# Value products of a pair of heads: second head first, the first head's ordered behind it

## The chip, the cores and the metric

The kernel runs on one core of a Trainium2 chip (trn2). The metric is the time of one execution on the device in microseconds. Before the change the median of three runs is 677.95 us (675.8 to 678.87).

The engines are named as the profile names them: PE is TensorE (its matmuls; PEld its weight loads), DVE is VectorE, ACT is ScalarE, POOL is GpSimd, SP is the engine whose queue issues the transfers.

## The reference

Three layers follow each other, for 4 batches of 576 positions. The first is causal attention with 8 heads of width 64 and a decaying bias, and it is the one that the change touches:

```python
scores = scale * np.matmul(q, k.transpose(0, 1, 3, 2))
cum = np.cumsum(np.maximum(s, 0.0), axis=-1)
bias = -(cum[:, :, :, None] - cum[:, :, None, :])
scores = np.where(causal, -1000000000.0, scores + np.minimum(bias, 0.0))
attn = np.exp(scores - np.max(scores, axis=-1, keepdims=True))
attn = attn / (np.sum(attn, axis=-1, keepdims=True) + 1e-09)
return np.matmul(attn, v)
```

The second layer is a gated expert (512 to 1024 wide, a gelu, a normalization, a product over positions `w_sg`, a product `w_out`, a residual). The third mixes neighbouring positions, has a product `w_k` with a squared relu, a product `w_v`, and a gate `w_r`.

## The kernel before

**Attention in pairs.** `attn_pair(b, hp)` treats two heads of a batch, so there are 16 pairs, numbered 0 to 15, four to a batch. For each block of 128 queries it makes the scores of a head (`sc`, lines 255 and 256, two matmuls each), VectorE adds the mask and finds the minimum (line 280), ScalarE takes the exponent and the row sums (line 288), TensorE transposes the result (`tp`, lines 303, 306 and 314), and ScalarE or VectorE copies it into the pair's probabilities `pt1` and `pt2` (lines 308 to 317). The steps run first over head 0, then over the last 64 queries of both heads, then over head 1.

**The value products** (lines 328 to 341) come last. They have two stages: `r = 0` makes the first 256 query columns from two blocks of keys, `r = 1` the other 320 from five blocks. In a stage each block of keys has one product for each head: the weights are the head's values (128 keys by 64), the moving operand its probabilities, and the result goes to partitions 0 to 63 of the accumulator `pv` for head 0 and to 64 to 127 for head 1. A first stage therefore has 4 products (256, 256, 128 and 128 columns), a second stage 10 (six of 320, two of 192, two of 64). ScalarE then copies the accumulator into `x_t` (line 343), and later VectorE multiplies it by the reciprocals of the row sums (line 355). The sums reach that place by a transpose (`rt`, line 320), an addition and a reciprocal on VectorE, and a trip through memory (`rdram`).

**The other work.** `moe1(b)` is the second layer of a batch. `gemm3` (line 371) issues all its matmuls: `v`, `u`, `sg` (the product over positions, the gating product below) and `o`. The attention of a batch is emitted in pieces between the matmuls of the layer two of the batch before, by the due times of `attention_until`. When attention has ended, its memory goes to the weights of the third layer, whose products `k`, `r` and `ps` fill the rest of the span.

**What sets the order.** The code is not run as it is written: a scheduler puts each engine's instructions in an order of its own, by simulated times, the dependences between tiles, and the order of emission where several could go. Its result is what an engine then works through from first to last. `after(late, early)` adds a dependence without a semaphore: `late` may not stand ahead of `early` on their engine.

Of the kernel before, what the change touches and what calls it, by code (L numbers as in the profile page):

```python
# [38 lines left out]
def fused_kernel(ctx, tc, kqT, vL, s, w_in, g_ln, w_sgT, b_sg, w_out, mu_k, mu_r, w_k, w_v, w_r, out):  # L39
    nc = tc.nc  # L40
# [170 lines left out]
    def attn_pair(b, hp):  # L211
# [3 lines left out]
        for hh in range(2):  # L215
# [24 lines left out]
            if hh == 0:  # L240
                vf = at.tile([P, 2, NT, D], F32, tag="vf", name=f"vf{pr}", bufs=2)
# [18 lines left out]
        for hh, i in steps:  # L260
# [8 lines left out]
            for ci, (c0, c1) in enumerate(chunks):  # L269
                sc = psum1.tile([P, 512], F32, tag="sc", name=f"sc{pr}_{hh}_{i}_{ci}", bufs=3)  # L270
                n = c1 - c0
# [58 lines left out]
        for r in range(2):  # L330
            q0, n = ((0, QS), (QS, S - QS))[r]
            acc = psum1.tile([P, 512], F32, tag="acc", name=f"pv{pr}_{r}", bufs=3)
            nk = 2 if r == 0 else NT
            for kk in range(nk):
                o = max(0, kk * P - q0)
                for a in range(2):
                    if r == 0:
                        pt = pt1[:, a, :QS] if kk == 0 else pt1[:, a, QS:]
                    else:
                        pt = pt2[:, a, kk, o:] if kk < 4 else pt2[:, a, 3, 0:64]  # L340
                    nc.tensor.matmul(acc[64 * a:64 * a + 64, o:n], vf[:, a, kk], pt, start=(kk == 0), stop=(kk == nk - 1))  # L341

            nc.scalar.copy(x_t[:, q0:q0 + n], acc[:, :n])  # L343
            yield 4000
# [144 lines left out]
    def after(late, early):  # L489
        tc.add_manual_dep(late.ins, early.ins.name, mybir.DependencyInfo(mybir.DependencyClass.NoSync, mybir.DependencyReason.DATA),  # L490
                          reason="order")
# [23 lines left out]


    pairs = [attn_pair(b, h) for b in range(B) for h in range(H // 2)]

    def a_stream():
# [83 lines left out]
    def dense(name, w, x, m, n):  # L603
        acc = bank(name)
        f = slice(m * P, (m + 1) * P)
        mms = []
        for k in range(KD):
            xh, xl = (x[:, i, k, :n] for i in range(2))
            mms += [(w[0][:, k, f], xh), (w[0][:, k, f], xl), (w[1][:, k, f], xh)]
        gemm3(acc[:, :n], mms)  # L610
        return acc[:, :n]
# [57 lines left out]
    for c, (t0, n) in enumerate(TILES):  # L669
        nxt = mixed(c + 1, 0, lk) if c + 1 < len(TILES) else mixed(0, 1, lk)  # L670
        for hg in range(4):
            t = kp.tile([P, 2, CH], F32, tag="t", name=f"k2_{c}_{hg}", bufs=2)[:, :, :n]
            for i in range(2):
                acc = dense(f"k{c}_{hg}_{i}", wk, x, 2 * hg + i, n)
# [66 lines left out]
    for c, (t0, n) in enumerate(TILES):  # L741
# [9 lines left out]
        for h in range(2):  # L751
            g = va.tile([P, 2, CH], F32, tag="g", name=f"g{c}_{h}", bufs=2)[:, :, :n]
            for i in range(2):
                acc = dense(f"r{c}_{h}_{i}", wr, x, 2 * h + i, n)
# [21 lines left out]
    for p in range(TOK // PW):  # L776
# [7 lines left out]
        a, b, c = (psum2.tile([P, 2, 512], F32, tag="ps", name=f"ps{n}_{p}", bufs=4) for n in "abc")  # L784
# [80 lines left out]
```

## Time and profile before

| | |
|---|---|
| median of three runs | 677.95 us (675.8 to 678.87) |
| profiled execution | 676.04 us, its span 674.3 us |
| TensorE matmuls | 639.1 us (95%), 3912 records |
| VectorE | 476.5 us (71%) |
| ScalarE | 413.5 us (61%) |
| GpSimd | 216.9 us (32%) |
| value products (line 341) | 448 records, 65.2 us busy, from 28.4 to 373.4 us |

Busy times on TensorE overlap (a matmul's recorded end is modelled, and the next one has begun by then), so how long a group really took is read from its start to the start of what follows, or from the chain of waits, whose pieces do not overlap. The granted clock is 1.00 from 60 us on; before, it is at the lower level for a part of the time.

### The profile page before, as it was taken

To read this page: it belongs to the slowest core of one execution; us is meant where nothing else is said; L and a number is where in the kernel's file an instruction comes from. 1 tells how busy PE (TensorE), PEld (TensorE's weight loads), DVE (VectorE), ACT (ScalarE), POOL (GpSimd) and SP (SyncE) were. 2 spreads that over 40 slices of the span, in tenths; PEclk is the share of its full clock that TensorE was granted. 3 is DMA by queue.
4 is the path that set the end of the run, shared out by engine and by line. 5 is a ranking of instruction groups with operands and counts; after the bars stand their busy time and mean duration, and the time that the engine had idled before them with its cause. 6 is when DMAs were issued, how large, how long until landed. Compare 5 with 4: busy or idle time off the path is not lost.

```text
span 674.3 us, 11528 instructions
## 1 busy us (share of the span) xinstructions
PE 639.1 (95%) x3912; PEld 553.3 (82%) x3912; DVE 476.5 (71%) x995; ACT 413.5 (61%) x940; POOL 216.9 (32%) x233
## 2 busy tenths in 40 slices
PE   2769999899999999999999999999999999999997
PEld 1556777779878988978988889988888988999997
DVE  6877489997668735559744388887875959677773
ACT  5868787884558646458643376577755779543530
POOL 7546636657446378345454030000000000000000
PEclk9879999999999999999999999999999999999999
DMA  7566563544654550842600674576645594546543
GB/s 221 149 200 210 140 194 88 167 141 154 182 173 109 151 140 22 239 150 72 158 29 7 238 275 164 155 229 222 243 163 184 182 359 146 172 179 201 222 141 117
DMA packets 56459, 112.74 MB, mean 167 GB/s; under 512 B 7680, under 2 KB 20624, under 8 KB 56400
## 3 DMA queue, kind: packets, MB, share of 16 engines
q1 hardware_dynamic: 56400, 112.01, 52.1%
q8 instruction: 31, 0.51, 0.3%
q14 instruction: 28, 0.23, 0.1%
HBM read 74.46 MB, written 28.02 MB: 152 GB/s over the span
## 4 chain that ended last, share of the span: by engine, by line
PE 57%; DMA 4%; DVE 2%; ACT 1%; issue 0%; SPq 0%; POOL 0%; DVEq 0%
PE k L371 14%; PE r L371 7%; PE psa L774 7%; PE sg L371 6%; PE o L371 4%; PE psb L774 4%; PE pv L341 3%; PE u L371 2%; PE v L371 2%; PE psc L774 2%; PE tp L306 2%; DMA wc<-wscr 2%; PE sc L255 1%; PE sc L256 1%; DMA lraw<-in_w_k_dram 1%; DMA rdram<-rc 0%
## 5 line engine op out<-in xcount | busy, mean ns | idle before, releaser
L371 PE MATMUL k<-x,wk 128*128 128x512 f32 (+1 forms) x480 | 99.1, 368 | 0.0
L371 PEld LDWEIGHTS k<-x,wk 128*128 128x128 f32 x480 | 83.6, 189 | 15.2 <-ACT x L599 0.3
L255 PE MATMUL sc<-ka,qa 128*128 128x512 f32 (+3 forms) x180 | 62.6, 361 | 20.6 <-ACT wv L88 11.7
L288 ACT ACTIVATE st<-st,mx 128x128 f32<-128x128 f32 (+4 forms) x124 | 71.9, 582 | 11.9 <-DVE mx L280 10.4
L280 DVE CUSTOM_DVE_ANT_0 st<-sc,mask 128x512 f32<-128x512 f32 (+3 forms) x124 | 60.7, 501 | 17.7 <-PE sc L256 8.7
L341 PE MATMUL pv<-pt,vf 128*64 128x320 f32 (+4 forms) x448 | 65.2, 367 | 0.3 <-ACT xT L343 0.3
L371 PE MATMUL sg<-wsg,vn 128*128 128x288 f32 x448 | 64.0, 298 | 0.0
L371 PEld LDWEIGHTS sg<-wsg,vn 128*128 128x128 f32 x448 | 60.4, 188 | 0.6 <-DVE pt L310 0.2
L255 PEld LDWEIGHTS sc<-ka,qa 128*128 128x128 f32 x180 | 33.3, 187 | 31.3 <-ACT wv L88 11.7
L256 PE MATMUL sc<-KB,QB 128*128 128x512 f32 (+3 forms) x180 | 56.8, 337 | 0.5 <-DMA KB<-crt 0.5
L341 PEld LDWEIGHTS pv<-pt,vf 128*64 128x64 f32 x448 | 35.1, 137 | 24.7 <-issue 7.6
L306 PE MATMUL tp<-ident,st 128*128 128x128 f32 x300 | 49.5, 282 | 3.0 <-DVE pt L317 2.6
L371 PE MATMUL r<-x,wr 128*128 128x512 f32 (+1 forms) x240 | 49.5, 368 | 0.0
L371 PE MATMUL v<-wv,xs 128*128 128x512 f32 x192 | 49.1, 399 | 0.1
L371 PEld LDWEIGHTS r<-x,wr 128*128 128x128 f32 x240 | 41.9, 189 | 7.5
L70 POOL TENSOR_TENSOR KB<-kq,ka 64x576 fp32r<-64x576 f32 x29 | 43.6, 1503 | 9.7 <-DVE ka L233 3.4
L70 POOL TENSOR_TENSOR qa<-kq,QB 64x576 fp32r<-64x576 f32 x29 | 43.7, 1507 | 4.6 <-ACT QB L232 2.5
L306 PEld LDWEIGHTS tp<-ident,st 128*128 128x128 f32 x300 | 37.3, 145 | 8.7 <-ACT pt L308 3.9
L371 PE MATMUL u<-xs,wc 128*128 128x288 f32 x288 | 42.5, 298 | 1.1 <-DMA wc<-wscr 1.1
L232 POOL CAST QB<-kq 64x576 fp32r<-64x576 f32 x28 | 19.4, 692 | 73.0 <-PE sc L256 48.5
L371 PE MATMUL o<-gh,wc 128*128 128x288 f32 x192 | 40.8, 298 | 0.3 <-DMA wc<-wscr 0.3
L371 PEld LDWEIGHTS v<-wv,xs 128*128 128x128 f32 x192 | 34.9, 188 | 7.4 <-DVE y L480 0.5
(188 smaller groups left out, 1451.3 us busy)
## 6 DMA issues: line engine op xcount, KB each, us to landing
wc<-wscr SPq DMA_DIRECT2D x24, 512.0 KB
kq<-in_kqT_dram SPq DMA_DIRECT2D x32, 288.0 KB
kr<-kdram SPq DMA_DIRECT2D x12, 768.0 KB
kdram<-k SPq DMA_DIRECT2D x16, 512.0 KB
yt<-ydram SPq DMA_DIRECT2D x24, 257.0 KB
vf<-in_vL_dram SPq DMA_DIRECT2D x16, 320.0 KB
ydram<-y SPq DMA_DIRECT2D x16, 288.5 KB
gt<-gdram SPq DMA_DIRECT2D x12, 384.0 KB
```

What stands on the lines that cost most here:

```text
L70: eng.tensor_tensor(out=lo, in0=x, in1=f32(hi), op=ALU.subtract)
L232: (nc.scalar.copy if hd < 2 else nc.gpsimd.tensor_copy)(qb[64:128], kq[64:128])
L255: nc.tensor.matmul(sc[:m, :c1 - c0], qa[:, q], ka[:, c0:c1], start=True, stop=False)
L256: nc.tensor.matmul(sc[:m, :c1 - c0], qb[:, q], kb[:, c0:c1], start=False, stop=True)
L280: mi = nc.vector.tensor_tensor_reduce(out=st[:, c0:c1], in0=sc[:, :n], in1=mk, op0=ALU.add, op1=ALU.min, scale=-SCALE, scalar=mx[:, 0:1] i ...
L288: e = nc.scalar.activation(st[:, :w], st[:, :w], AF.Exp, bias=mx[:, last:last + 1], scale=-1.0, accum_out=sm[:, i + 5 * (hh == 1):i + 5 * ...
L306: nc.tensor.transpose(tp[:, c:c + P], st[:, j * P:(j + 1) * P], ident)
L341: nc.tensor.matmul(acc[64 * a:64 * a + 64, o:n], vf[:, a, kk], pt, start=(kk == 0), stop=(kk == nk - 1))
L371: nc.tensor.matmul(acc, a, w_, start=(i == 0), stop=(i == n - 1))
L774: nc.tensor.matmul(ps[:, c, :HW], l, r, start=(start and i == 0), stop=(i == len(mms) - 1), skip_group_check=True)
```

## The change

For each block of keys the product of head 1 is emitted first and that of head 0 second, and a dependence without a semaphore keeps head 0's behind head 1's on TensorE. This holds for both stages and all 16 pairs. Products of different blocks, other work between two products, and everything else are left to the scheduler as before.

```diff
-                for a in range(2):
+                both = []
+                for a in (1, 0):
                     if r == 0:
                         pt = pt1[:, a, :QS] if kk == 0 else pt1[:, a, QS:]
                     else:
                         pt = pt2[:, a, kk, o:] if kk < 4 else pt2[:, a, 3, 0:64]
-                    nc.tensor.matmul(acc[64 * a:64 * a + 64, o:n], vf[:, a, kk], pt, start=(kk == 0), stop=(kk == nk - 1))
+                    both.append(nc.tensor.matmul(acc[64 * a:64 * a + 64, o:n], vf[:, a, kk], pt, start=(kk == 0), stop=(kk == nk - 1)))
+                after(both[1], both[0])
```

Two lines are added, so line 341 of the kernel before is line 342 of the changed one, and line 371 is line 373.

The first place is TensorE around the value products of pair 14, with 16 pairs in all. `pv14_0` and `pv14_1` are the accumulators of its first and second stage, `sc15` scores of the next pair, `tp14` a transpose, `rt14` the transpose of the sums, `sg2` the gating product of batch 2. Before:

```order
L341 MATMUL pv14_0_4286<-pt1_14_4085,vf14_4070 64x256
L255 MATMUL sc15_2_4_0_4470<-ka31_4398,qa31_4397 128x512
...
L306 MATMUL tp14_1_3_4270<-ident_66,st14_1_3_4243 128x128 x4
L341 MATMUL pv14_0_4286<-pt1_14_4085,vf14_4070 64x256
L341 MATMUL pv14_0_4286<-pt1_14_4085,vf14_4070 64x128 x2
...
L341 MATMUL pv14_1_4308<-pt2_14_4086,vf14_4070 64x320
L255 MATMUL sc15_2_4_1_4476<-ka31_4398,qa31_4397 128x64
...
L341 MATMUL pv14_1_4308<-pt2_14_4086,vf14_4070 64x320 x5
L341 MATMUL pv14_1_4308<-pt2_14_4086,vf14_4070 64x192 x2
L341 MATMUL pv14_1_4308<-pt2_14_4086,vf14_4070 64x64 x2
```

The same place now:

```order
L306 MATMUL tp14_1_3_4270<-ident_66,st14_1_3_4243 128x128 x4
L342 MATMUL pv14_0_4286<-pt1_14_4085,vf14_4070 64x256 x2
L342 MATMUL pv14_0_4286<-pt1_14_4085,vf14_4070 64x128 x2
L320 MATMUL rt14_4276<-ident_66,sums0_96 9x128
L373 MATMUL sg2_0_1_4292<-wsg0_99,vn0_2_3645 128x288
...
L342 MATMUL pv14_1_4308<-pt2_14_4086,vf14_4070 64x320 x6
L342 MATMUL pv14_1_4308<-pt2_14_4086,vf14_4070 64x192 x2
L342 MATMUL pv14_1_4308<-pt2_14_4086,vf14_4070 64x64 x2
```

In each stage one product stood apart, ahead of the others; now both stages stand in one piece, behind the last transposes of head 1. In the order before, a product stands apart in the first stage of pairs 0, 3, 4, 5 and 9 to 15 and in the second stage of pairs 0, 1, 2, 3, 4, 8, 9, 12, 13 and 14, and pair 7's second stage is cut after five products. In the order now, only pair 7's second stage is cut, after six.

The second place is TensorE at the start of pair 8's scores. `sc8_0_0_0` is their first accumulator, `tp7` and `tq7` are transposes of pair 7, `sg0_0_1` and `sg0_1_0` gating products of batch 0. Before:

```order
L341 MATMUL pv6_1_1782<-pt2_6_1524,vf6_1508 64x320 x6
L341 MATMUL pv6_1_1782<-pt2_6_1524,vf6_1508 64x192 x2
L341 MATMUL pv6_1_1782<-pt2_6_1524,vf6_1508 64x64 x2
L306 MATMUL tp7_2_4_1958<-ident_66,st7_2_4_1942 128x128 x4
L314 MATMUL tq7_1963<-ident_66,st7_2_4_1942 128x128
L255 MATMUL sc8_0_0_0_2193<-ka16_2167,qa16_2166 128x128
L256 MATMUL sc8_0_0_0_2193<-KB0_90,QB0_88 128x128
```

The same place now:

```order
L306 MATMUL tp7_0_3_1936<-ident_66,st7_0_3_1912 128x128 x4
L255 MATMUL sc8_0_0_0_2193<-ka16_2167,qa16_2166 128x128
L373 MATMUL sg0_0_1_1766<-wsg0_99,vn0_0_1030 128x288
...
L342 MATMUL pv6_1_1782<-pt2_6_1524,vf6_1508 64x320 x6
L342 MATMUL pv6_1_1782<-pt2_6_1524,vf6_1508 64x192 x2
L342 MATMUL pv6_1_1782<-pt2_6_1524,vf6_1508 64x64 x2
L306 MATMUL tp7_2_4_1958<-ident_66,st7_2_4_1942 128x128 x4
L314 MATMUL tq7_1963<-ident_66,st7_2_4_1942 128x128
L256 MATMUL sc8_0_0_0_2193<-KB0_90,QB0_88 128x128
```

The first matmul of pair 8's scores has moved ahead of 14 gating matmuls, of pair 6's second stage and of five transposes; its second matmul has stayed behind them.

## Rows read from the trace of the kernel before

**Rows 1.** The page: busy us, share of the span, instructions.

```profile
PE 639.1 (95%) x3912; PEld 553.3 (82%) x3912; DVE 476.5 (71%) x995; ACT 413.5 (61%) x940; POOL 216.9 (32%) x233
```

**Rows 2.** Stretches: length, each engine's busy us, TensorE's granted clock, DMA share, GB/s.

```profile
28.00:84.00 56.00, 47.03 (x292) 33.95 (x291) 39.01 (x100) 41.76 (x115) 34.35 (x28) 0.90 0.58 174
...
100.00:160.00 60.00, 55.45 (x383) 47.49 (x382) 56.10 (x137) 48.40 (x136) 37.88 (x38) 1.00 0.49 148
160.00:375.00 215.00, 214.30 (x1465) 182.70 (x1465) 126.58 (x340) 119.19 (x308) 114.06 (x121) 1.00 0.41 119
```

**Rows 3.** TensorE's waits (sum, times, longest): 28-160, 160-375, 376-674 us.

```profile
PE sc L255 <- DVE mx L280: 6.4, 6, 3.0
PE tp L306 <- DVE pt L317: 2.6, 1, 2.6
...
PE sc L255 <- POOL xs L70: 0.4, 1, 0.4
PE pv L341 <- ACT xT L343: 0.3, 1, 0.3
...
PE u L371 <- DMA wc<-wscr: 1.1, 1, 1.1
```

**Rows 4.** The chain of waits around pair 14: start, length, what.

```profile
338.15 0.58 PE pv L341 x2
...
340.28 0.80 PE pv L341 x5
...
343.25 0.68 PE pv L341 x2
...
344.72 2.20 PE pv L341 x16
```

**Rows 5.** TensorE in order of time, pairs 7 and 10: start, length, what.

```profile
165.91 0.87 PE L341 MATMUL pv<-pt,vf 128*64 128x256 f32 x8
166.71 0.40 PE L371 MATMUL o<-gh,wcs 128*128 128x288 f32 x1
...
170.79 1.83 PE L341 MATMUL pv<-pt,vf 128*64 128x320 f32 x10
172.54 0.53 PE L371 MATMUL o<-gh,wcs 128*128 128x288 f32 x2
173.01 1.19 PE L341 MATMUL pv<-pt,vf 128*64 128x320 f32 x10
174.13 0.44 PE L306 MATMUL tp<-ident,st 128*128 128x128 f32 x2
...
245.26 2.27 PE L341 MATMUL pv<-pt,vf 128*64 128x320 f32 x20
247.46 0.80 PE L371 MATMUL sg<-wsg,vn 128*128 128x288 f32 x4
```

**Rows 6.** The chain of waits: three transposes at two places.

```profile
289.19 0.48 PE tp L306 x3
...
314.55 0.33 PE tp L306 x3
```

**Rows 7.** The chain of waits: the first stage of pair 15.

```profile
367.49 0.58 PE pv L341 x3
...
368.27 0.36 PE pv L341 x2
```

**Rows 8.** TensorE in order of time, pair 1 behind pair 0's first stage.

```profile
32.44 0.30 PE L303 MATMUL tp<-ident,st_f 128*128 128x128 f32 x1 [1.62 <-DVE rc L322]
```

**Rows 9.** TensorE in order of time, ahead of pair 8's scores.

```profile
147.47 2.11 PE L371 MATMUL sg<-wsg,vn 128*128 128x288 f32 x14
...
152.23 0.30 PE L255 MATMUL sc<-ka,qa 128*128 128x128 f32 x1
```

**Rows 10.** GpSimd in order of time: pair 8's operand.

```profile
148.08 1.51 POOL L70 TENSOR_TENSOR qa<-kq,QB 64x576 fp32r<-64x576 f32 x1
```

## The prediction, made before the changed kernel was timed

> **What bounds the kernel now.** I read the page first, to find the busiest engine [rows 1]: TensorE's matmuls fill 639.1 of 674.3 us, VectorE 476.5. A share of the whole span hides stages, so next I cut it at the places where the value products stand [rows 2]. The reader is to see three stretches. From 28 to 84 us (attention of the first batch, nearly alone) TensorE is busy 47.03 of 56 us, at a mean granted clock of 0.90. From 100 to 160 it has 55.45 of 60, but VectorE has 56.10 of 60. From 160 to 375, where the attention of batches 1 to 3 is threaded through the first expert's matmuls, TensorE has 214.30 of 215 us at full clock, while VectorE has 126.58. There TensorE's own time is the bound. The waits say the same from the other side [rows 3]: 6.4 us (3.0 of them at once) and 2.6 for VectorE before 160 us; the only two from 160 to 375 are 0.4 and 0.3 us.
>
> So a microsecond of matmul time taken out between 160 and 375 us should come off the end; one taken out earlier may be swallowed by a wait for VectorE.
>
> **What a value product costs.** Each product leaves two records (two passes). The chain of waits around pair 14 [rows 4], whose order stands in the first two fences of the section on the change, shows this. Head 0's first product of the first stage stands alone: two records, 0.58 us. What is left of that stage takes 0.80 us. Then head 0's first product of the second stage, alone again: 0.68 us, and what is left of that stage 2.20 us. Now the groups that were not cut [rows 5]: the first stage of pair 7, all 8 records, takes 166.71 - 165.91 = 0.80 us; the second stage of pair 10, all 20 records, takes 247.46 - 245.26 = 2.20 us. A cut group therefore takes as long, after its first product has gone, as a whole group does. The reading: the two heads write the two halves of the output's partitions, and each half runs its own string of products beside the other. In a whole group the strings are equally long. When head 0 has gone ahead with one product, head 1's string is still whole and sets the length; what head 0 did ahead was done alone and bought nothing.
>
> A lone product also makes its neighbours slower: three transposes take 0.48 us between two lone products, and 0.33 us after other work [rows 6], so 0.15 us more. I take 0.58 + 0.15 = 0.73 us for a lone product of the first stage and 0.68 + 0.15 = 0.83 for one of the second.
>
> The Trainium skill has a rule that speaks against this: "TensorE: Matmul & The Clock Gate", Part 3, "What overlaps and what doesn't", says that a weight load overlaps running matmuls only where the row group differs. Both heads use all 128 rows and differ in columns alone. By that rule the heads would run one behind the other, a whole group would take longer than a cut one's remainder, and the main term below would shrink to its neighbours, 12 x 0.15 = 1.8 us. The rows disagree: both take 2.20 us.
>
> **The change part by part.** It adds and removes no instruction and no transfer, and changes no tile. Head 1's product comes first, and head 0's may not pass it. Head 0's probabilities are ready before head 1's, which is how they could go ahead; now nothing of a group can go before head 1's are there. The new order on TensorE has every group whole except pair 7's second stage, which two other matmuls cut after three key blocks, between full rounds.
>
> From 160 to 375 us the order before has lone first-stage products in pairs 9 to 15: 7 x 0.73 = 5.1 us. Pair 15's remainder is also cut, by the transpose of the sums (0.58 + 0.36 instead of 0.80 [rows 7]): 0.15. Lone second-stage products stand in pairs 8, 9, 12, 13 and 14: 5 x 0.83 = 4.15. Pair 7's second stage is cut after five products: 172.54 - 170.79 plus 174.13 - 173.01 is 2.87 us instead of 2.20 [rows 5]: 0.67. Together 10.1 us, and what stands right behind them is more matmul work, so nothing hides it.
>
> From 84 to 160 us: pair 4 loses one of each (1.56), pair 5 one of the first stage (0.73): 2.3 us. VectorE is late next there (56.10 of 60 us). The ends are 0 and 2.3; I take 0.8, nearer to the VectorE row.
>
> From 28 to 84 us: pairs 0 and 3 lose one of each (3.1), pairs 1 and 2 a second-stage product that stood right behind a whole first stage, 0.53 each: 4.2 us. But TensorE waits here anyway. In pair 0 the two lone products stand ahead of the transpose of the sums, whose reciprocal then ends a wait of 1.62 us [rows 8]: that wait should end 0.58 + 0.68 = 1.3 us sooner. Ends: 4.2 above; below, the clock. The mean of 0.90 over 56 us [rows 2] is 11 us at the lower of its two levels (1.2 of 2.4 GHz); half as much again (5.6 us) would cost 2.8. I take a gain of 1.0, near the waits' row.
>
> Waits of the new order: it moves other work too. The place I can price is the first score product of pair 8. Before, it stands behind the second group of pair 6 and starts at 152.23; now it stands ahead of 14 matmuls of the gating product, of that group and of five transposes, which start at 147.47 [rows 9]. Its operand is written by GpSimd, which ends at 148.08 + 1.51 = 149.59 [rows 10]. TensorE takes its matmuls in order, so about 2.1 us would be spent waiting, and the gating matmuls queued behind it, and VectorE behind them, would wait too. Ends for all such waits together: a gain of 0.7 (all that is waited now from 160 to 375) and a loss of 5.6 (the two longest waits before 160 once more, 3.0 and 2.6 [rows 3]). I take a loss of 2.0, the one place found.
>
> After 375 us: a chain runs from pair 15's sums over their trip through memory to the loads of the next batch's weights, and TensorE waits 1.1 us for one of these [rows 3]. The sums move with the matmuls before them, so I take 0 (ends: 0, and a gain of 1.1).
>
> Sum: 10.1 + 0.8 + 1.0 - 2.0 = 9.9 us. The profiled execution took 676.04 us, 1.7 more than its span: 666.1. It was 1.9 us below the median of the runs shown, from which the same step leads to 668.1. I forecast 667.
>
> **The rivals.**
> (a) Part of it is swallowed: VectorE, which makes the scores' exponents ready and scales the result, ends some waits after 160 us. For: it sets the pace from 100 to 160. Against: 126.58 of 215 us. At half the main term: 671.
> (b) Slower, by in-order waits: the scheduler places score products before their operands are there, in pair 8 and again in pairs 9 to 15. At 2.1 us for each of the eight, 17 us of waits against 11.9 of gain: 681. It decides from 1.5 us of new waits per pair on. Against: in the old order, by the same scheduler, the one wait of a score product after 160 us is 0.4.
> (c) The two heads run beside each other only when head 0 leads. Then each pair's two groups double: 0.80 + 2.20 = 3.0 us for each of 12 pairs after 84 us, against 10.1: 702. Against: in a cut group head 1 is the one that lags a product behind, so its strings start out of step, and still nothing is lost.
> (d) Everything comes through, the early stretches and the end too, and no new wait: 10.1 + 2.3 + 4.2 + 1.1 = 17.7 from the profiled run: 658.
>
> **How the numbers follow.** The forecast has 0.66 (its own range 662 to 671), (a) 0.16, (b) 0.08, (c) 0.03, (d) 0.07. The range that should hold 8 in 10 goes from 660 to 674: the forecast, most of (a), part of (d). 0.5%, 3.4 us, is about what a measurement of this kernel can tell from no change. Faster by more: the forecast, (d) and ten of (a)'s sixteen hundredths: 0.83. Within: the rest of (a) and three hundredths of (b): 0.09. Slower: the rest of (b), and (c): 0.08.
>
> **What would show it.** Right: in pairs 0 to 15 no two records of a value product alone; each second stage 20 records in about 2.2 us, each first stage 8 in 0.8; TensorE still full from 160 us to the end of attention, which comes some 9 to 10 us sooner. Wrong: whole groups of 4 us (c); TensorE waits of a microsecond or more in front of score products (b), first of all pair 8's; or a longer stretch at the lower clock before 84 us.

## The result and the profile after

The changed kernel takes 668.26 us (median of 6 runs, 665.15 to 672.16); the kernel before, run beside it, 677.13 us (6 runs, 675.80 to 678.87). The ratio is 0.987 with a 95% interval of 0.9839 to 0.9901: faster by 8.9 us. The profiled execution of the changed kernel took 665.15 us with a span of 663.4 (before: 676.04 and 674.3). It is the shortest of its six, so the profile shows 10.9 us where the medians show 8.9.

The page and the stretches of the changed kernel, which answer to [rows 1, 2]:

```profile
PE 625.9 (94%) x3912; PEld 549.2 (83%) x3912; DVE 479.1 (72%) x995; ACT 413.2 (62%) x940; POOL 220.3 (33%) x233
```

```profile
28.00:84.00 56.00, 45.19 (x294) 33.54 (x295) 39.32 (x104) 42.62 (x116) 34.67 (x29) 0.91 0.62 184
100.00:160.00 60.00, 55.33 (x395) 48.44 (x394) 55.69 (x136) 48.06 (x132) 36.94 (x36) 1.00 0.48 149
160.00:375.00 215.00, 212.13 (x1509) 185.93 (x1508) 130.57 (x345) 120.66 (x312) 113.61 (x121) 1.00 0.43 128
```

The same 3912 matmul records keep TensorE busy for 13.2 us less. The reader is to see the third stretch: 1509 records fit where 1465 did, while TensorE now idles 2.9 us of it instead of 0.7.

TensorE in order of time, pairs 7, 10 and 14 and the first stage of pair 15 (start, length, what), to set beside [rows 4, 5, 7]:

```profile
168.05 1.83 PE L342 MATMUL pv<-pt,vf 128*64 128x320 f32 x12
169.82 0.53 PE L373 MATMUL o<-gh,wcs 128*128 128x288 f32 x2
170.28 0.66 PE L342 MATMUL pv<-pt,vf 128*64 128x192 f32 x8
...
239.70 2.27 PE L342 MATMUL pv<-pt,vf 128*64 128x320 f32 x20
...
332.53 0.87 PE L342 MATMUL pv<-pt,vf 128*64 128x256 f32 x8
...
335.40 2.27 PE L342 MATMUL pv<-pt,vf 128*64 128x320 f32 x20
...
355.47 0.87 PE L342 MATMUL pv<-pt,vf 128*64 128x256 f32 x8
```

No pair of records stands alone any more. Pair 14's first product no longer costs 0.58 and 0.68 us ahead of its two groups, and what is left is no longer than it was: in the chain of waits 0.80 and 2.20 us before, 0.80 and 2.21 now. Pair 7's second stage, cut between full rounds, takes 169.82 - 168.05 plus 170.87 - 170.28 (the start of what follows) = 2.36 us instead of 2.87.

The waits of TensorE (sum, times, longest) in 28 to 160, 160 to 360 and 360 to 663 us, beside [rows 3]:

```profile
PE tp L303 <- DVE rc L322: 3.8, 1, 3.8
PE sc L255 <- DVE mx L280: 2.6, 5, 1.3
PE sc L255 <- DMA ka<-ka: 2.3, 2, 1.5
...
PE tp L306 <- ACT u L504: 1.6, 1, 1.6
...
PE tp L306 <- DVE pt L317: 1.2, 2, 0.9
PE tq L314 <- DVE pt L310: 1.0, 2, 0.7
PE sc L255 <- DVE mx L280: 0.3, 1, 0.3
...
PE o L373 <- DMA wc<-wscr: 0.8, 1, 0.8
```

Two places of the early part, which answer to [rows 8, 9]:

```profile
31.50 0.30 PE L303 MATMUL tp<-ident,st_f 128*128 128x128 f32 x1 [3.77 <-DVE rc L322]
...
32.27 3.92 PE L342 MATMUL pv<-pt,vf 128*64 128x320 f32 x20
...
144.82 0.30 PE L255 MATMUL sc<-ka,qa 128*128 128x128 f32 x1 [1.51 <-DMA ka<-ka]
144.95 2.08 PE L373 MATMUL sg<-wsg,vn 128*128 128x288 f32 x14
146.96 2.28 PE L342 MATMUL pv<-pt,vf 128*64 128x320 f32 x20
```

The wait ahead of pair 1's transposes ends 0.94 us sooner, not 1.3, and is 3.77 us long instead of 1.62: the two lone products that used to fill it have gone behind it. Right after it pair 0's second stage takes 3.92 us, not the 2.28 of later pairs, and the granted clock is 0.54 from 32.5 to 35.9 us:

```profile
32.50:35.90 3.40, 3.40 (x16) 1.59 (x16) 2.88 (x4) 1.08 (x3) 1.73 (x1) 0.54 1.00 329
```

**Where the 10.9 us come from.** Three marks that both traces have: pair 4's second stage, pair 7's second stage, and the second run of matmuls of `k`. Before, then after:

```profile
92.38 2.27 PE L341 MATMUL pv<-pt,vf 128*64 128x320 f32 x18
...
436.19 4.04 PE L371 MATMUL k<-x,wk 128*128 128x512 f32 x17
```

```profile
91.18 2.28 PE L342 MATMUL pv<-pt,vf 128*64 128x320 f32 x20
...
425.29 14.93 PE L373 MATMUL k<-x,wk 128*128 128x512 f32 x65
```

Pair 4's second stage starts 1.2 us sooner, pair 7's 170.79 - 168.05 = 2.74 us sooner [rows 5], `k` 10.90 us sooner, and so does the end. Between the last two marks 10.90 - 2.74 = 8.16 us are gained although TensorE's gaps there grew from 2.2 to 3.7 us: those up to 360 us by 2.2, while the two waits for `wc` (1.1 and 0.3) became one of 0.8. The matmul work taken out there is 8.16 + 1.5 = 9.6 us. The groups of value products themselves, each from its start to the start of what follows, give 8.0 of it.

Not all of the first 1.2 us is the change's. TensorE works through the same order in both kernels up to the first value product, and yet it starts a score product ahead of it 0.95 us sooner, before and after:

```profile
24.82 0.30 PE L255 MATMUL sc<-ka_f,qa_f 128*128 128x128 f32 x1 [2.14 <-DMA ka_f<-ka_f]
```

```profile
23.87 0.30 PE L255 MATMUL sc<-ka_f,qa_f 128*128 128x128 f32 x1 [0.92 <-DMA ka_f<-ka_f]
```

In the other executions profiled the same product starts between 23.67 and 25.68 us. So 0.95 of the 10.9 us stood in the profile before any product had changed its place.

### The profile page after: what moved, and what is told of

It reads as the page before. It is cut to its first block, busy times and chain, and to the rows that moved or that the text cites. A ratio compares the mean times of both kernels' runs of the same rounds, so it can differ in the third digit from the quotient of the medians.

```text
span 663.4 us, 11516 instructions
## 1 busy us (share of the span) xinstructions
PE 625.9 (94%) x3912; PEld 549.2 (83%) x3912; DVE 479.1 (72%) x995; ACT 413.2 (62%) x940; POOL 220.3 (33%) x233
## 4 chain that ended last, share of the span: by engine, by line
PE 70%; DVE 10%; DMA 8%; ACT 4%; SPq 3%; POOL 2%; issue 2%; DVEq 0%; ACTq 0%; POOLq 0%
PE k L373 15%; PE sg L373 9%; PE r L373 7%; PE o L373 7%; PE psa L776 7%; PE pv L342 4%; PE psb L776 4%; PE u L373 3%; PE tp L306 3%; DMA rb<-rdram 3%; PE sc L255 3%; PE v L373 3%; PE sc L256 3%; PE psc L776 2%; DVE st L280 1%
## 5 line engine op out<-in xcount | busy, mean ns | idle before, releaser
L255 PE MATMUL sc<-ka,qa 128*128 128x512 f32 (+3 forms) x180 | 62.2, 361 | 20.9 <-ACT wv L88 10.9
L255 PEld LDWEIGHTS sc<-ka,qa 128*128 128x128 f32 x180 | 33.9, 191 | 29.7 <-ACT wv L88 10.9
L342 PE MATMUL pv<-pt,vf 128*64 128x320 f32 (+4 forms) x448 | 52.2, 372 | 0.0
L306 PE MATMUL tp<-ident,st 128*128 128x128 f32 x300 | 48.0, 278 | 4.0 <-ACT u L504 1.6
L342 PEld LDWEIGHTS pv<-pt,vf 128*64 128x64 f32 x448 | 29.8, 139 | 21.3 <-issue 5.3
L70 POOL TENSOR_TENSOR qa<-kq,QB 64x576 fp32r<-64x576 f32 x29 | 43.7, 1509 | 4.0 <-ACT QB L232 1.9
L596 ACT ACTIVATE yx<-yt,mu 128x64 f32<-128x64 f32 (+4 forms) x64 | 30.6, 531 | 17.2 <-DMA yt<-ydram 17.1
L232 POOL CAST QB<-kq 64x576 fp32r<-64x576 f32 x28 | 21.4, 764 | 59.0 <-PE sc L256 34.5
```

The lines of the kernel that those rows point to most:

```text
L70: eng.tensor_tensor(out=lo, in0=x, in1=f32(hi), op=ALU.subtract)
L232: (nc.scalar.copy if hd < 2 else nc.gpsimd.tensor_copy)(qb[64:128], kq[64:128])
L255: nc.tensor.matmul(sc[:m, :c1 - c0], qa[:, q], ka[:, c0:c1], start=True, stop=False)
L306: nc.tensor.transpose(tp[:, c:c + P], st[:, j * P:(j + 1) * P], ident)
L342: both.append(nc.tensor.matmul(acc[64 * a:64 * a + 64, o:n], vf[:, a, kk], pt, start=(kk == 0), stop=(kk == nk - 1)))
L596: i = nc.scalar.mul(t[:, s0:s1], yt[:, s0 + d:s1 + d], mu[:, r, 1, k:k + 1])
```

## The experiments

To compare orders that differ everywhere, I divide one stretch of each profiled execution, from 28 us to the first matmul of `k` (430.70 us before, 419.48 after), into three: gaps between one matmul's end and the next's start; half of the time that TensorE is busy at the lower clock, which is what half speed costs it; and the rest, which is matmul work at full clock. From that first matmul of `k` to the end of the span it is 243.1 to 244.1 us in every kernel. All are worked out from the matmul rows and the granted clock. The median is of all runs of a kernel; the columns behind it are of one execution, whose time stands beside and can lie several us off the median (4.5 above it with the second stage alone). The two executions of the changed kernel have the same work, 367.8 us.

| kernel | median us | execution shown, us | first `k` | gaps | half of busy time at lower clock | work |
|---|---|---|---|---|---|---|
| before | 677.13 | 676.04 | 430.7 | 15.7 | 4.4 | 382.6 |
| changed | 668.26 | 665.15 | 419.5 | 19.0 | 4.7 | 367.8 |
| changed, once more | 667.4 | 667.58 | 422.5 | 19.7 | 7.0 | 367.8 |
| head 0 first, groups whole | 673.67 | 673.48 | 428.3 | 20.4 | 7.2 | 372.7 |
| batches 1 to 3 alone | 672.27 | 674.81 | 429.5 | 20.1 | 8.7 | 372.6 |
| batch 0 alone | 680.08 | 683.21 | 437.7 | 17.8 | 12.8 | 379.2 |
| first stage alone | 670.4 | 670.54 | 425.7 | 15.9 | 4.3 | 377.5 |
| second stage alone | 683.02 | 687.49 | 442.3 | 26.1 | 11.1 | 377.1 |
| heads one after the other | 701.98 | 701.93 | 456.0 | 13.8 | 2.9 | 411.4 |
| pair 8's product back | 666.92 | 667.99 | 422.4 | 19.2 | 6.1 | 369.2 |
| sums in their own bank | 673.36 | 676.55 | 431.2 | 26.5 | 8.1 | 368.7 |
| own bank and pair 8 | 674.58 | 667.86 | 422.7 | 18.3 | 7.0 | 369.3 |

My theory was the prediction's: whole groups save the lone products, whatever makes them whole, and what is saved behind 160 us comes off the end. The rivals were that head 1 must lead, that only some part of the change matters, and that the time came from the reordering around it.

**Whole groups with head 0 leading.** Head 0 stays first, as in the kernel before, and in the scheduler's order a first stage's first product is held behind the last copy of head 1's probabilities, a second stage's behind ScalarE's copy of the first stage's result. Against the kernel before:

```diff
-                (nc.vector.tensor_copy if i == 3 and not first else nc.scalar.copy)(
+                cpl = (nc.vector.tensor_copy if i == 3 and not first else nc.scalar.copy)(
...
-                    nc.tensor.matmul(acc[64 * a:64 * a + 64, o:n], vf[:, a, kk], pt, start=(kk == 0), stop=(kk == nk - 1))
-
-            nc.scalar.copy(x_t[:, q0:q0 + n], acc[:, :n])
+                    mm = nc.tensor.matmul(acc[64 * a:64 * a + 64, o:n], vf[:, a, kk], pt, start=(kk == 0), stop=(kk == nk - 1))
+                    if a == kk == 0:
+                        after(mm, cpl)
+
+            cpl = nc.scalar.copy(x_t[:, q0:q0 + n], acc[:, :n])
```

> Head 0's products are emitted first as before, but its first product of a stage is held (in the scheduler's order only) until head 1's last probabilities are copied, so that from pair 4 on no stage has a lone product, with head 0 leading. Theory (lone products cost their own time, who leads is indifferent): as after the change, 666 to 669 us, each whole second stage 2.20 us. Rival (head 1's lead is what makes the two run side by side, or what shortens the wait): 675 to 678 us.

673.67 us (12 runs, 670.36 to 676.17), ratio 0.994 (0.992 to 0.9959). Neither expectation was met. Its groups are as fast as those of the changed kernel:

```profile
339.44 0.87 PE L341 MATMUL pv<-pt,vf 128*64 128x256 f32 x8
343.66 2.27 PE L341 MATMUL pv<-pt,vf 128*64 128x320 f32 x20
```

So which head leads makes no difference to a group's length. Its work is 10.0 us below before's. It has 4.7 us more gaps and 2.8 more for the clock, and pairs 0 to 3 are still cut. The edit is not a test of the leading head alone: by its second hold, pair 14's second stage starts 4.22 us after its first (343.66 - 339.44) and not 2.87 (335.40 - 332.53), and whether that made the new gaps is not shown.

**Batches 1 to 3 alone, and batch 0 alone.** From the changed kernel, with the added dependence in the same pairs only; for batch 0 alone the two orders are swapped.

```diff
-                for a in (1, 0):
+                for a in ((0, 1) if first else (1, 0)):
```

> The change in pairs 4 to 15 only; pairs 0 to 3 as before. Theory (the gain comes where TensorE is full, the early stretch swallows its part): 666 to 669 us. Rival (the gain comes from the first batch, everything behind it moving up): 673 to 677 us.

672.27 us (11 runs, 670.59 to 676.08), ratio 0.9939 (0.9915 to 0.9963).

> The change in pairs 0 to 3 only; from pair 4 on the lone products stand as before (seven in first stages and five in second stages after 160 us). Theory: 674 to 677 us, a gain of 0 to 2 us of the 4.2 us of lone products removed. Rival (first batch is the source): 667 to 670 us.

680.08 us (12 runs, 677.02 to 683.21), ratio 1.0036 (1.0015 to 1.0057).

Both medians lie 3 us above the expected range. Their work is 10.0 and 3.4 us less than before, 13.4 together, and the whole change has 14.8: the removed work nearly adds up. What came on top is new waits and stretches at the lower clock. In the kernel with batches 1 to 3 alone, TensorE in order of time at two waits, and the stretches behind them (the first of them behind three shorter waits of 1.13, 0.75 and 0.56 us, the last of which ends at 113.3 us):

```profile
215.65 0.84 PE L306 MATMUL tp<-ident,st 128*128 128x128 f32 x3 [1.96 <-DVE pt L317]
...
331.68 0.39 PE L314 MATMUL tq<-ident,st 128*128 128x128 f32 x1 [2.47 <-DVE pt L310]
```

```profile
113.40:116.80 3.40, 3.40 (x14) 2.04 (x15) 3.40 (x8) 3.25 (x11) 3.15 (x4) 0.51 0.39 121
215.80:219.20 3.40, 3.40 (x15) 2.20 (x14) 2.43 (x12) 3.21 (x11) 3.30 (x4) 0.51 0.38 100
331.80:335.20 3.40, 3.18 (x13) 2.91 (x13) 2.81 (x11) 3.27 (x11) 0.87 (x1) 0.50 0.01 2
```

A wait of 2 us there cost 3.7: its own length, and half of 3.4 us behind it. With batch 0 alone, two such stretches lie behind waits of 1.69 and 2.27 us; the first of them:

```profile
114.20:121.00 6.80, 6.35 (x24) 5.16 (x25) 5.72 (x20) 5.57 (x17) 2.04 (x5) 0.51 0.27 82
```

**One stage alone.** From the changed kernel, with the added dependence in that stage only. The line `for a in ((1, 0) if r == 0 else (0, 1))`, and the same with `r == 1`.

> The change in the first stages (256 columns) only. In the order this gives, no first stage has a lone product, and second stages have one in pairs 0 to 5 and 8 to 14: after 160 us seven instead of five. Theory (0.73 us for each lone product of a first stage, 0.83 for one of a second): 5.25 us gained less 2 x 0.83, so 3.6 us after 160 us, and about half a microsecond before: 672 to 674 us. Rival (the gain is in the waits and the moved work, not in counted products): no such sum; either as the full change, 667, or as before, 677.

670.4 us (6 runs, 667.85 to 670.9), ratio 0.9889 (0.9864 to 0.9914): better than expected.

> The change in the second stages (320 columns) only. In the order this gives, no second stage has a lone product (pair 7's is cut after two), and first stages have one in pairs 0, 2, 3, 4, 5, 7, 9 to 13 and 15. After 160 us: five second-stage products gone (4.15 us), pair 7's cut spared (0.67), first-stage ones seven as before. Theory: 4.8 us after 160 us, about half a microsecond before: 671 to 673 us. Rival as for the first stages: 667 or 677.

683.02 us (6 runs, 681.16 to 687.92), ratio 1.0096 (1.006 to 1.0132): a clear miss.

By work the two stages are near each other, 5.1 and 5.5 us. Together that is 10.6 and not 14.8, because each order has lone products of the other stage that the order before has not: three more second-stage ones with the first stage alone, one more first-stage one with the second. At the prediction's prices (3 x 0.83 and 0.73) they are 3.2 of the 4.2 us; the rest is open. The first stage alone has the waits and clock of before, and gains; the second alone has, in a slow one of its executions, 17.1 us more of both, and loses. TensorE there, with the clock around it:

```profile
136.65 0.45 PE L314 MATMUL tq<-ident,st 128*128 128x128 f32 x1 [3.64 <-DVE pt L310]
```

```profile
136.50:143.30 6.80, 6.49 (x27) 6.22 (x28) 4.52 (x15) 5.09 (x16) 2.83 (x2) 0.52 0.51 153
```

So half of the change, with half of its saving, can be slower than nothing, by where the scheduler then puts everything else. Why it puts the work so in this case was not found out.

**The heads one after the other.** All blocks of one head, then all of the other, so that hardly anything of a group can run side by side. Against the kernel before:

```diff
-            for kk in range(nk):
-                o = max(0, kk * P - q0)
-                for a in range(2):
+            for a in range(2):
+                for kk in range(nk):
+                    o = max(0, kk * P - q0)
```

> All products of head 0 in a stage, then all of head 1, so that no two products of different heads stand side by side. Theory (the two heads run beside each other, a stage takes one head's string): every whole stage doubles, 0.80 + 2.20 us for each of 12 pairs on top of 667, and part of four more: 700 to 712 us. Rival (heads never overlap; the change only spared neighbours and waits): the same columns in a different order, 674 to 680 us.

701.98 us (2 runs, 701.93 and 702.02), ratio 1.0359 (1.0326 to 1.0393), as expected. The second stage of pair 15 (pair 14's is as long):

```profile
367.23 3.94 PE L341 MATMUL pv<-pt,vf 128*64 128x320 f32 x20
```

The same 20 records, 3.94 us instead of 2.27, and 28.7 us more work than before. In other pairs the scheduler put the heads' strings apart, and one head's ten records alone take what both heads' twenty take:

```profile
214.55 2.27 PE L341 MATMUL pv<-pt,vf 128*64 128x320 f32 x10
```

So two heads in the two halves of the partitions do run side by side, weights and all, when their products alternate. The single records say it too: in pair 10 of the kernel before the two heads' weight loads, and their matmuls, start less than 0.01 us apart, and each head's next 320 columns start 0.27 us later, as in the string that runs alone. That is what a lone product gives up.

**Pair 8's product back.** Its first score product stands behind the transposes again; all else is in the order of the changed kernel.

```diff
-            nc.tensor.matmul(sc[:m, :c1 - c0], qa[:, q], ka[:, c0:c1], start=True, stop=False)
+            m0 = nc.tensor.matmul(sc[:m, :c1 - c0], qa[:, q], ka[:, c0:c1], start=True, stop=False)
+            if pr in HELD and q.start == 0 and hh == 0:
+                after(m0, last_tq[0])
...
-                nc.tensor.transpose(tp4[:, 0:P], st[:, 512:640], ident)
+                last_tq[0] = nc.tensor.transpose(tp4[:, 0:P], st[:, 512:640], ident)
...
+    HELD = (8,)
```

> The changed kernel with one instruction put back: the first score product of pair 8 is held behind the last transpose of pair 7, where it stood before the change; no other instruction changes its place on any engine. Theory (the 1.51 us that TensorE waits there for the copy of ka are lost for good): the wait goes, and the time falls by 0.5 to 1.5 us against the changed kernel. Rival (GpSimd and VectorE set the pace there, and the wait comes back in front of a later instruction before 160 us): 0 us.

666.92 us (5 runs, 664.38 to 667.99), ratio 0.9838 (0.9813 to 0.9864). The wait of 1.51 us is gone from its place; the gating products, pair 6's second stage and the next gating products now stand so:

```profile
146.52 2.13 PE L376 MATMUL sg<-wsg,vn 128*128 128x288 f32 x14 [0.53 <-DVE u L510]
148.57 2.28 PE L345 MATMUL pv<-pt,vf 128*64 128x320 f32 x20
152.47 2.11 PE L376 MATMUL sg<-wsg,vn 128*128 128x288 f32 x14 [0.47 <-ACT xT L348]
```

Two waits of 0.5 us stand in its stead, so about 0.5 us of the 1.51 could come of it at that place. The median is 0.5 below that of the changed kernel run beside it (667.4), which lies within the spread of either: whether the wait costs anything at the end is not shown.

**The changed kernel once more.** No edit.

> The changed kernel once more, as the measure for the others of this call: 665 to 672 us as in its first six runs, and a profile whose waits of the first batch may differ, since the granted clock of those six runs went from 0.981 to 0.992. If the clock of the first batch makes that spread, a slower run has a longer stretch at the lower level before 84 us and the same times after it.

667.4 us (6 runs, 664.68 to 669.65), ratio 0.985 (0.9824 to 0.9875). In both profiled executions TensorE waits 1.64 us for `u` on ScalarE at the same place. Here is the stretch from 111.4 us, in the first profile and then in this one:

```profile
111.40:114.80 3.40, 3.40 (x25) 2.72 (x26) 3.32 (x11) 3.40 (x12) 3.00 (x4) 1.00 0.37 102
```

```profile
111.40:114.80 3.40, 3.40 (x15) 2.04 (x15) 3.32 (x11) 3.19 (x12) 2.80 (x4) 0.53 0.42 119
```

The same instructions behind the same wait ran 25 records in one and 15 in the other. The clock can fall in one execution of a program and not in another, at a price of 1.7 us. The expectation, that a slower execution differs before 84 us alone, held in part: from 28 to 84 us the lower clock takes 13.7 us here and 10.2 in the first, and this one stretch comes on top.

**The sums in a bank of their own.** Pair 0's transposed sums take an accumulator's bank, so that pair 1's transposes need not wait for VectorE to read them. This is aimed at the 3.77 us.

```diff
-        rt = psum1.tile([P, 512], F32, tag="tp", name=f"rt{pr}", bufs=2)
+        rtag = "acc" if pr == 0 else "tp"
+        rt = psum1.tile([P, 512], F32, tag=rtag, name=f"rt{pr}", bufs=3 if rtag == "acc" else 2)
```

> As the changed kernel, but the transposed sums of pair 0 go into an accumulator's bank of PSUM instead of one of the two that the transposes use, so that pair 1's first transposes need not wait for VectorE to have read them. Theory (the time of this change that is not matmul work lies in waits, and in the lower clock behind them): the wait of 3.77 us ahead of pair 1's transposes goes or shrinks below 1 us, and the 1.7 us at the lower clock right behind it with it; 2 to 5 us less than the changed kernel, 662 to 665 us, if no wait of over 1.5 us comes elsewhere. Rival (VectorE, which runs that reciprocal late because it is full, sets the pace of the first batch): the wait moves to the next transposes or scores that need VectorE; 667 to 669 us.

673.36 us (6 runs, 672.66 to 676.55), ratio 0.9945 (0.9923 to 0.9966): slower than the changed kernel, and beyond the rival too. TensorE in order of time:

```profile
31.47 2.28 PE L343 MATMUL pv<-pt,vf 128*64 128x320 f32 x20 [1.67 <-DVE rc L323]
...
41.32 0.69 PE L255 MATMUL sc<-ka,qa 128*128 128x384 f32 x1 [3.58 <-DVE mx L280]
```

Up to here the edit does what it was made for: pair 0's second stage waits only 1.67 us, runs at full clock, and ends at 33.67, 2.45 us sooner than in the changed kernel. But at 41.32 a wait for VectorE's minimum ends that is 3.58 us long; the changed kernel's wait ahead of the same product is 1.28 us and ends at 40.28:

```profile
40.28 0.44 PE L255 MATMUL sc<-ka,qa 128*128 128x384 f32 x1 [1.28 <-DVE mx L280]
```

Two waits of 3.77 and 1.28 have become 1.67 and 3.58, and the lead has turned into a lag of 1.04 us. The clock is low for 10.2 us from 38.0 us on, 0.3 us into this wait:

```profile
38.00:48.20 10.20, 5.95 (x21) 4.86 (x22) 8.04 (x22) 6.61 (x18) 4.63 (x5) 0.50 0.58 174
```

That wait is not TensorE's to take away: VectorE, which has to make the minimum, itself stands 2.98 us there, ahead of a cast:

```profile
40.16 0.90 DVE L233 CAST ka_f<-kq 64x576 fp32r<-64x576 f32 x1 [2.98 <-DMA rb<-rdram]
```

The profile names a transfer of the sums (`rb`), the last to land, but the cast reads `kq`, whose transfer was issued at 35.11; which of the two held it is open. So TensorE did not set the pace here, and the time freed on it turned into a wait a few us on. The further loss, the gaps of 84 to 160 us (9.1 instead of 5.3) and after (5.5 instead of 2.9), came with the new order.

**Both edits.**

> Both edits at once: the transposed sums of pair 0 in a bank of their own, and the first score product of pair 8 behind the transposes that it stood ahead of. The order before 60 us is to be that of the kernel with the first edit alone. Theory of waits: 0 to 1.5 us less than with the first edit alone, 661 to 665 us. Rival (orders differ by up to some us in waits and clock that no edit here aims at): anywhere from 664 to 672 us, with a wait of 1.5 us or more at a place that neither edit touches.

674.58 us (12 runs, 667.86 to 677.32), ratio 0.9953 (0.9934 to 0.9972): again beyond the rival. Its profiled execution is its best, with a clock of 0.986 over the whole span; that at 677.32 has 0.979, that at 676.11 has 0.971. One program differs by 9.5 us from execution to execution.

Not run: the change without its added dependence, since every engine's order is then the same row for row. The order of emission alone makes the groups whole, and products into one accumulator keep the order in which they are written.

No version beats the changed kernel by more than a measurement can tell.

## Why the prediction was right

**The main term held.** 10.1 us of work were to go from pair 7's second stage on, with nothing to hide them. By the marks 9.6 went, 8.0 of it in the value products; the other 1.6 is near the 12 x 0.15 = 1.8 that the prediction had for their neighbours, but was not taken apart. Its reading, that a lone product buys nothing since the other half's string stays whole, is shown by both leading heads (0.80 and 2.20 us) and by the serial kernel.

**All lone products together** were counted as 10.1 + 2.3 + 4.2 = 16.6 us; 14.8 of work went. In batch 0 alone it was 3.4 against 4.2 counted.

**The sum was helped by luck.** Up to pair 7's second stage the terms give 1.0 + 0.8 - 2.0 = -0.2 us, and behind it 10.1. In the profile 2.7 came before that mark, 0.95 of it from the start of the execution, and 8.2 behind it, where new waits took 1.5. Two errors of 2.9 and 1.9 us nearly cancel.

**28 to 160 us: swallowed in part.** The terms 1.0 and 0.8 stood against 6.5 that were counted; by the table 14.8 - 9.6 = 5.2 of work went there. By pair 4's second stage 1.2 had come, 0.25 without the head start of 0.95. From there to pair 7's second stage 1.5 came in spite of pair 8's wait of 1.5, so the second of the two terms was too small: VectorE's wait of 2.6 us at 135.5 [rows 3] is gone in the new order. For batch 0 the reason was right: VectorE is late next. Its detail was wrong: the wait ahead of pair 1's transposes was to end 1.3 us sooner because the sums are transposed sooner. They are, by 3.1 us (26.65 instead of 29.75), and it brings nothing: the wait ends 0.94 us sooner, which is the head start. VectorE in order of time in the changed kernel shows why:

```profile
24.47 0.29 DVE L280 CUSTOM_DVE_ANT_0 st_f<-sc,mask 128x128 f32<-128x128 f32 x1 [1.38 <-PE sc L256]
...
27.46 1.65 DVE L233 CAST ka<-kq 64x576 fp32r<-64x576 f32 x1
...
29.64 1.51 DVE L83 SCALAR_TENSOR_TENSOR syt<-sraw,syt 128x512 uint32<-128x512 uint32 x1
31.08 0.27 DVE L322 TENSOR_SCALAR rc<-rt 9x128 f32<-9x128 f32 x1
```

The addition to the sums (line 322) stands at 31.08 behind an unbroken row of other work, a cast of 1.65 us and an operation on `syt` of 1.51 among it; that row set the time, not the transpose. In the kernel before, VectorE works through the same row 0.95 us later, from 25.42 us on. The feared longer stretch at the lower clock did not come (0.91 against 0.90).

**New waits: 2.0 us predicted.** Pair 8's came where it was said, 1.51 us instead of 2.1, but that the sizes are near is luck: another operand was the late one. By the profile a transfer of `ka` ended it, and GpSimd's last write of a `qa` before it, which answers to [rows 10], ended at 141.21, 8.4 us sooner than the 149.59 of the old order that the price was worked out from:

```profile
139.79 1.42 POOL L70 TENSOR_TENSOR qa<-kq,QB 64x576 fp32r<-64x576 f32 x1
```

It was not the one place: 1.64 us for ScalarE at 110.72, and 2.0 us more in short waits from 160 to 360. All gaps together up to `k` grew by 3.3 us, within the bounds and above the value taken.

**After 375 us: 0.** The waits for `wc` there went from 1.1 and 0.3 to 0.8. Attention's last group starts 11.6 us sooner (359.75 instead of 371.35), not 9 to 10, and `k` follows 10.9 sooner.

**The rivals.** (a) had VectorE end waits after 160: it did, for 2.5 of the 200 us to 360, far from half of the main term. (b) fell: the score products of pairs 9 to 15 wait 0.3 us in all. (c) fell with the groups' lengths. (d) fell by the waits.

So the number is right for the reason given, but less firmly than it looks. What was removed is worth 14.8 us; two kernels that remove 10 us of it in another order gain only 3.5 and 5. Gaps and clock lie between 16.7 and 37.2 us in these kernels, by an order that no view of the profile before shows. That the new order had only 3.6 us more of both than the old one was not worked out, and the prediction could not have worked it out.

## What to carry to other kernels

Look in the trace for products that write one half of the output's partitions and stand apart from their partners in the other half: each costs its whole length, and here emitting the operand that is ready last first was enough to keep the pairs together. Count such work only where TensorE has no gaps; where another engine sets the pace, a wait takes its place. And where a scheduler makes the order, expect some us of noise in waits and clock for any edit, so measure an edit's parts as well as the whole.

## What the runs showed that was not expected

- Behind TensorE's waits of 1.6 to 3.8 us in the middle of the kernel the granted clock often went to the lower of its two levels (1.2 of 2.4 GHz) and stayed there for some us, 3.4 to 10.2 on end. Such a wait costs its length and half of that stretch. Between 28 us and `k` the half makes 2.9 to 12.8 us in these kernels.
- It need not happen: the same order behind the same 1.64 us kept the full clock in one execution and fell to 0.53 in another, and behind 3.02 us at 342.66 in the kernel with the second stage alone it did not fall. It is part of why one program's runs differ by 3 to 10 us.
- An edit that removes matmul work can come with more time at the lower clock: the second stage alone saves 5.5 us of work and, in the execution shown, has 6.7 us more for the clock and 10.4 more gaps.
- The same order can start an execution a microsecond sooner or later: the changed kernel and the one with pair 8's product back are to have the same order, but for one product, and by 25 us they are 1 us apart.
